# One of eight tiles transposed by PE inside a product, in a spectral filter, soft mixture and SoLU kernel

## The chip, the cores and the metric

The kernel runs on one core of one Trainium2 chip. Its engines are PE (the matmul array, with its weight loads listed apart as PEld), DVE (vector), ACT (scalar), POOL (GpSimd) and SP, which here only issues DMAs. Each engine takes its instructions in the order in which the program lists them and waits on semaphores where data come from another. The metric is device microseconds; the time is the median of several runs.

## The reference

```
X = rfft(x over 3072 positions)          # x: 8 x 3072 x 256
Y = softshrink(complex X @ (w_r, w_i) + b);  x = irfft(Y)     # 24576 tokens of 256
# soft mixture: 32 slots of 8 experts, dispatch and combine by softmax of x @ phi
x = combine @ experts(dispatch.T @ x)    # w1, w2 with relu
h = x @ w_in                             # 24576 x 1024
solu = h * softmax(h)
ln = (solu - mean) / sqrt(var + 1e-6) * g_ln
out = ln @ w_out                         # 24576 x 256
```

## The kernel before

A first phase (to some 660 us of the profile) does the filter, the statistics of the mixture and the combine weights, which it writes to memory as c. The change lies in the second phase, the function phase2: 192 tiles of 128 tokens. The experts' outputs times w_in are one 128 x 1024 matrix (gst), so a tile's hidden values are one product of c with it.

For a tile t these are the operations, with the name of the function that issues them:
- hmat: two matmuls of 512 columns into hps, 128 x 1024 in PSUM. There are three such buffers.
- rowmax (DVE): a reduction over hps. gst has its sign turned, so the minimum is taken.
- expo (ACT): the exponential e of hps, with its sum.
- umul (DVE): u = hps times e, with its sum. It is the last reader of hps.
- vari (ACT): the square of u less its mean, only for its sum.
- blocks: DVE transposes u in blocks of 32 x 32 into tb, and SP issues four DMAs that move whole blocks within the chip's memory, so that t2 holds u with hidden features on partitions.
- uhi and ulo: f32 is split into a rounded part uh (f32r, ACT for 768 columns, POOL for 256) and a rest ul (POOL, two subtractions of 512 columns).
- prod: 24 matmuls of 256 columns into po, in f32r: uh with the high and with the low part of gw (w_out scaled by g_ln, split likewise), and ul with the high part. po holds two tiles to a buffer and has two buffers.
- rstd (POOL, four small operations to four tiles) and outp (ACT): the product scaled into osb; store writes four tiles' osb out.

The last two tiles are "direct": their u is transposed by PE (trans), for which the columns of their hidden values are put in another order by the matrix gstn. load_c brings c for coming tiles, four DMAs to eight tiles.

All this is issued from one hand-written loop. In step i it issues hmat(i+3), rowmax(i+2), umul(i+1), blocks(i+1), store, load_c, outp(i-6), vari(i), expo(i+2), uhi(i-1), ulo(i-1), rstd(i) and prod(i-3), and no scheduler changes the order. An engine therefore runs its part of this list in order, and a wait on it delays all that stands behind.

Of the kernel before, what the change touches and what calls it, by code (L numbers as in the profile page):

```python
# [8 lines left out]
F32 = mybir.dt.float32  # L9
F32R = mybir.dt.float32r  # L10
# [3 lines left out]
AF = mybir.ActivationFunctionType  # L14
ALU = mybir.AluOpType
# [20 lines left out]
def kernel(  # L36
# [24 lines left out]
    PE, ACT, DVE, POOL, SP = nc.tensor, nc.scalar, nc.vector, nc.gpsimd, nc.sync  # L61
    B, N, D = x.shape
# [5 lines left out]
    DFF = 1024  # L68
    NI = T // 128
# [18 lines left out]
    def mm(out, lhsT, rhs, start=True, stop=True):  # L88
        PE.matmul(out=out, lhsT=lhsT, rhs=rhs, start=start, stop=stop)  # L89

    def tp(out, in_, k=128):
        PE.transpose(out=out, in_=in_, identity=ident[0:k, 0:k])  # L92
# [752 lines left out]
    def phase2(p2: ExitStack, pw: ExitStack):  # L845
        k_p = p2.enter_context(tc.tile_pool(name="k2_p", bufs=1))
        c_p = p2.enter_context(tc.tile_pool(name="c_p", bufs=1))

        gw = k_p.tile([128, 8, 2, D], F32R, name="gw")
        gw_h, gw_l = gw[:, :, 0, :], gw[:, :, 1, :]  # L850
        gst = k_p.tile([128, DFF], F32R, name="gst")
        gstn = k_p.tile([128, DFF], F32R, name="gstn")
        cts = {}


# [8 lines left out]
        p = ExitStack()  # L864
# [5 lines left out]
        ps = pt.tile([128, 2, 32], F32, name="pslt", tag="pt")  # L870
# [66 lines left out]
        for fh in range(2):  # L937
            n = 0
# [13 lines left out]
        def right(name, bufs, **k):  # L952
            return p2.enter_context(tc.tile_pool(name=name, bufs=bufs, side="right", **k))

        e_p = right("e_p", 2)
        u_p = right("u_p", 4)
        o_p = right("o_p", 2)
# [3 lines left out]
        po_p = right("po_p", 2, space=PSUM)  # L961
        NG = NI // 4
        ctt, hps, et, ut, uht, stt, osb, pot = {}, {}, {}, {}, {}, {}, {}, {}
# [13 lines left out]
        def hmat(i):  # L977
            if i >= NI:
                return
            j, k = divmod(i, 4)  # L980
            ps = ph_p.tile([128, DFF], F32, name="hps", tag="hps")
            for fh in range(2):
                mm(ps[:, 512 * fh:512 * fh + 512], ctt[j][:, 128 * k:128 * k + 128], (gstn if direct(i) else gst)[:, 512 * fh:512 * fh + 512])
            hps[i] = ps

        def stats(i):
            j, k = divmod(i, 4)
            if k == 0 and j not in stt:
                stt[j] = s_p.tile([128, 6, 4], F32, name="st", tag="st")
            return stt[j], k  # L990

        def rowmax(i):
            if i >= NI:
                return
            st, k = stats(i)
            DVE.tensor_reduce(out=st[:, 0, k:k + 1], in_=hps[i], op=ALU.min, axis=AX.X)  # L996

        def expo(i):
            if i >= NI:
                return  # L1000
            st, k = stats(i)
            e = e_p.tile([128, DFF], F32, name="e", tag="e")
            ACT.activation(out=e, in_=hps[i], func=AF.Exp, bias=st[:, 0, k:k + 1], scale=-1.0, accum_out=st[:, 1, k:k + 1])  # L1003
            et[i] = e

        def umul(i):
            if i >= NI:
                return
            st, k = stats(i)
            u = u_p.tile([128, DFF], F32, name="u", tag="u")  # L1010
            DVE.scalar_tensor_tensor(out=u, in0=hps.pop(i), scalar=1.0, in1=et.pop(i), op0=ALU.mult, op1=ALU.mult, accum_out=st[:, 2, k:k + 1])  # L1011
            ut[i] = u


        def direct(i):
            return i >= NI - 2

        def gst_order():
            POOL.tensor_copy(out=gstn.rearrange("p (c j b) -> p b c j", c=8, b=4), in_=gst.rearrange("p (b c j) -> p b c j", b=4, c=8).bitcast(F32))

        def blocks(i):
            if i >= NI or direct(i):
                return
            t = u_p.tile([128, DFF], F32, name="tb", tag="tb", bufs=3)
            DVE.transpose(out=t, in_=ut[i])  # L1027
            t2 = u_p.tile([128, 4, 256], F32, name="t2", tag="t2", bufs=3)
            for a in range(4):
                z = slice(32 * a, 32 * a + 32)  # L1030
                SP.dma_start(out=t2[:, a, :], in_=t[z].rearrange("i (b x) -> i b x", b=4))  # L1031
            t2t[i] = t2

        def trans(i):
            if i >= NI or not direct(i):
                return
            ps = ph_p.tile([128, 8, 128], F32, name="pu", tag="hps")
            for c in range(8):
                tp(ps[:, c, :], ut[i][:, 128 * c:128 * c + 128])
            ut[i, 0] = ps  # L1040

        def parts(i):
            uh = u_p.tile([128, 8, 128], F32R, name="uh", tag="uh")
            ul = u_p.tile([128, 8, 128], F32R, name="ul", tag="ul")
            uht[i] = (uh, ul)
            return uh, ul
# [9 lines left out]
                DVE.tensor_tensor(out=ul[:, z, :], in0=ps[:, z, :], in1=uh[:, z, :].bitcast(F32), op=ALU.subtract)  # L1056


        HA = 6

        def uhi(i):
            if i < 0 or direct(i):
                return
            uh, ul = parts(i)
            v = t2t[i].rearrange("p a (c j) -> p c a j", c=8)
            w = uh.rearrange("p c (a j) -> p c a j", a=4)
            ACT.activation(out=w[:, 0:HA], in_=v[:, 0:HA], func=AF.Copy)  # L1067
            POOL.tensor_copy(out=w[:, HA:8], in_=v[:, HA:8])  # L1068

        def ulo(i, n):  # L1070
            if i < 0 or direct(i):
                return
            uh, ul = uht[i]
            z = slice(4 * n, 4 * n + 4)
            v = t2t[i].rearrange("p a (c j) -> p c a j", c=8)[:, z]
            w = uh[:, z, :].rearrange("p c (a j) -> p c a j", a=4)
            POOL.tensor_tensor(out=ul[:, z, :].rearrange("p c (a j) -> p c a j", a=4), in0=v, in1=w.bitcast(F32), op=ALU.subtract)  # L1077
            if n:
                t2t.pop(i)


        def vari(i):
            if i >= NI:
                return
            st, k = stats(i)
            sq = e_p.tile([128, DFF], F32, name="sq", tag="sq", bufs=1)
            ACT.activation(out=sq, in_=ut.pop(i), func=AF.Square, bias=st[:, 2, k:k + 1], scale=-float(DFF), accum_out=st[:, 3, k:k + 1])  # L1087

        def prod(i):
            if i < 0 or i >= NI:  # L1090
                return
            uh, ul = uht.pop(i)
            if i % 2 == 0:
                pot[i // 2, 0] = po_p.tile([128, 2, D], F32, name="po2", tag="po2")
            ps = pot[i // 2, 0][:, i % 2, :]
            for f in range(8):
                mm(ps, uh[:, f, :], gw[:, f, 0, :], f == 0, False)
                mm(ps, uh[:, f, :], gw[:, f, 1, :], False, False)
            for f in range(8):
                mm(ps, ul[:, f, :], gw[:, f, 0, :], False, f == 7)  # L1100
            pot[i] = ps


        def rstd(i):
# [9 lines left out]
            POOL.tensor_tensor(out=st[:, 3, k], in0=st[:, 3, k], in1=st[:, 1, k], op=ALU.add)  # L1114
            POOL.tensor_tensor(out=st[:, 4, k], in0=st[:, 3, k], in1=mhalf[:, k], op=ALU.pow)

        o_todo = {}

        def outp(i):
            if i < 0:  # L1120
                return
            j, k = divmod(i, 4)
            b, r = divmod(j, 6)
            h, ah = divmod(r, 2)
            v = out.rearrange("(b h lm a) d -> b h lm a d", b=B, h=3, a=8)[b, h, :, 4 * ah:4 * ah + 4, :]
            if k == 0:
                osb[0] = o_p.tile([128, 4, D], F32, name="osb", tag="osb")
            o = osb[0]
            ACT.activation(out=o[:, k], in_=pot.pop(i), func=AF.Copy, scale=stt[j][:, 4, k:k + 1])  # L1129
            if j == NG - 1:  # L1130

                SP.dma_start(out=v[:, k, :], in_=o[:, k, :])
            elif k == 3:
                o_todo[i + 2] = (v, o)


        def store(i):
            if i in o_todo:
                v, os2 = o_todo.pop(i)
                SP.dma_start(out=v, in_=os2)  # L1140
# [20 lines left out]
        def late_c(i):  # L1161
            if i in c_todo:
                load_c(*c_todo.pop(i))
# [5 lines left out]
        for i in range(3):  # L1169
            hmat(i)  # L1170
# [5 lines left out]
        blocks(0)  # L1176
        for i in range(NI + 6):
            j, k = divmod(i, 4)
            hmat(i + 3)
            trans(i)  # L1180
            rowmax(i + 2)
            umul(i + 1)
            blocks(i + 1)
            store(i - 6)
            late_c(i)
            last_c(i)
            outp(i - 6)
            vari(i)
            expo(i + 2)
            direct_parts(i)  # L1190
            if i <= NI:
                uhi(i - 1)
                ulo(i - 1, 0)
            rstd(i)
            if i <= NI:
                ulo(i - 1, 1)
            if i == 40:
                gst_order()
            if k == 1:
                pieces(j + 2)  # L1200
            prod(i - 3)
        while o_todo:
            store(min(o_todo))

# [139 lines left out]
```

## Time and profile before

| | |
|---|---|
| time, median of 3 runs | 1365.99 us (1365.64 to 1366.42) |
| profiled execution, first to last instruction | 1364.4 us |
| busy: PE, PEld, DVE, ACT, POOL | 1268.9, 1126.9, 1207.1, 1038.8, 979.4 us |
| mean granted clock of PE | 0.981 of 2.4 GHz |
| DMA, mean | 185 GB/s |

The profile is of one execution, and its own time is the span of 1364.4 us; the median of the runs is 1.6 us above it. The busy times are sums over the whole span, over two phases with different limits, so they do not say what bounds the second. A matmul's duration includes its way through the array; the distance between the starts of two is what each costs in a row of them. The same holds in part on DVE and ACT, whose instructions overlap a little.

### The profile page before, as it was taken

What the parts mean: (1) busy time and instruction counts of PE and PEld (TensorE: products, weight loads), DVE (VectorE), ACT (ScalarE), POOL (GpSimd) and SP (SyncE); (2) the same over time, 40 slices, a digit from 0 to 9 for tenths busy, and PEclk for the clock granted to TensorE, in tenths of its full rate; (3) what the DMA queues carried; (4) which work ended last, traced back from release to release, by engine and by line L of the source; (5) the groups of instructions that cost most, each with busy time, mean ns of one, the idle gap of its engine ahead of it and who ended that gap; (6) DMA issues with size and microseconds to landing.
All of it is one profiled execution on the core that took longest, in us unless ns stands there. A gap on an engine that the chain in (4) does not pass through costs nothing.

```text
span 1364.4 us, 30891 instructions
## 1 busy us (share of the span) xinstructions
PE 1268.9 (93%) x10784; PEld 1126.9 (83%) x10784; DVE 1207.1 (88%) x1691; ACT 1038.8 (76%) x2005; POOL 979.4 (72%) x1045
## 2 busy tenths in 40 slices
PE   6999999999999999878699989999999999899998
PEld 3888888888878788855588888988898889888897
DVE  7787988888888989765999999999999999999994
ACT  5567665666667665533799889999899999899995
POOL 5557575757565654221588989989899999889996
PEclk8899999999999999999799999999999999999999
DMA  8966463646445464168478788778877888787874
GB/s 267 289 202 175 124 193 111 209 117 186 140 144 167 126 181 155 62 223 291 108 179 220 188 210 209 198 197 209 205 194 203 196 198 217 196 206 191 201 197 125
DMA packets 190746, 252.70 MB, mean 185 GB/s; under 512 B 21504, under 2 KB 155392, under 8 KB 190592
## 3 DMA queue, kind: packets, MB, share of 16 engines
q1 hardware_dynamic: 190256, 249.57, 67.3%
q8 instruction: 85, 1.39, 0.4%
q10 hardware_dynamic: 336, 1.18, 0.2%
q14 instruction: 69, 0.57, 0.1%
HBM read 91.94 MB, written 59.11 MB: 111 GB/s over the span
## 4 chain that ended last, share of the span: by engine, by line
PE 37%; POOL 14%; DMA 13%; issue 12%; DVE 10%; SPq 8%; ACT 6%; POOLq 0%; ACTq 0%; DVEq 0%
PE po L89 10%; DMA t<-tb 9%; POOL ul L1077 8%; PE pb L89 6%; PE pm L89 6%; SPq L1031 6%; PE s L89 4%; PE xps L89 4%; PE pa L89 3%; DMA xc<-in_x_dram 3%; POOL x L235 2%; PE sps L92 2%; SPq L861 2%; POOL uh L1068 2%; ACT uh L1067 1%
## 5 line engine op out<-in xcount | busy, mean ns | idle before, releaser
L1077 POOL TENSOR_TENSOR ul<-t,uh 128x512 fp32r<-128x512 f32 x380 | 486.1, 1296 | 31.8 <-ACT uh L1067 30.7
L89 PEld LDWEIGHTS po<-gw,uh 128*128 128x128 f32 x3072 | 384.9, 190 | 80.8 <-ACT osb L1129 72.2
L89 PE MATMUL po<-gw,uh 128*128 128x256 f32 x3072 | 404.9, 284 | 41.7 <-ACT osb L1129 41.4
L346 POOL TENSOR_TENSOR s<-yb,s 128x512 f32<-128x512 f32 x95 | 132.4, 1394 | 216.9 <-DVE s L345 187.8
L1027 DVE STREAM_TRANSPOSE tb<-u 128x1024 f32<-128x1024 f32 x190 | 236.7, 1246 | 7.0 <-DMA t<-tb 0.4
L1011 DVE SCALAR_TENSOR_TENSOR u<-hps,e 128x1024 f32<-128x1024 f32 x192 | 232.3, 1210 | 11.6 <-ACT e L1003 11.1
L996 DVE TENSOR_REDUCE st<-hps 128x1 f32<-128x1024 f32 x192 | 227.7, 1186 | 1.7 <-PE hps L89 1.7
L1087 ACT ACTIVATE sq<-u,st 128x1024 f32<-128x1024 f32 x192 | 221.3, 1152 | 0.2 <-DVE u L1011 0.2
L1003 ACT ACTIVATE e<-hps,st 128x1024 f32<-128x1024 f32 x192 | 214.1, 1115 | 7.2 <-DVE st L996 6.6
L89 PE MATMUL po<-gw,ul 128*128 128x256 f32 x1536 | 213.0, 281 | 0.8 <-POOL ul L1077 0.8
L89 PEld LDWEIGHTS po<-gw,ul 128*128 128x128 f32 x1536 | 195.3, 189 | 1.1 <-POOL ul L1077 1.0
L1067 ACT ACTIVATE uh<-t 128x768 fp32r<-128x768 f32 x190 | 160.5, 845 | 44.6 <-DMA t<-tb 41.1
L235 POOL TENSOR_TENSOR x<-xc,x 96x512 fp32r<-96x512 f32 x120 | 164.7, 1381 | 29.5 <-ACT x L234 28.4
L89 PE MATMUL hps<-gst,ct 128*128 128x512 f32 x380 | 119.5, 397 | 12.0 <-DVE u L1011 10.5
L261 ACT ACTIVATE asb<-s 96x512 f32<-96x512 f32 x112 | 66.6, 595 | 73.8 <-PE s L89 73.2
L89 PE MATMUL s<-x,df_h 96*96 96x512 f32 x240 | 105.0, 440 | 12.9 <-ACT x L234 4.6
L1068 POOL CAST uh<-t 128x256 fp32r<-128x256 f32 x190 | 75.9, 400 | 49.9 <-DMA t<-tb 46.3
L89 PEld LDWEIGHTS xps<-d_sb,apt 128*128 128x128 f32 x768 | 99.4, 194 | 14.1 <-issue 2.9
L89 PE MATMUL xps<-d_sb,apt 128*128 128x128 f32 x768 | 105.8, 281 | 2.1 <-DMA apt<-ad 1.6
L1129 ACT ACTIVATE osb<-po,st 128x256 f32<-128x256 f32 x192 | 89.5, 468 | 10.2 <-PE po L89 9.1
L234 ACT ACTIVATE x<-xc 96x512 fp32r<-96x512 f32 x120 | 75.1, 626 | 13.2 <-DMA xc<-in_x_dram 13.2
L297 DVE TENSOR_TENSOR xsum<-xps,xi 128x256 f32<-128x256 f32 x96 | 39.8, 414 | 47.9 <-ACT xh L296 44.8
(204 smaller groups left out, 2232.1 us busy)
## 6 DMA issues: line engine op xcount, KB each, us to landing
t<-tb SPq DMA_DIRECT2D x760, 128.0 KB, 2.8
apt<-ad SPq DMA_DIRECT2D x96, 256.0 KB, 4.2
out_dram<-osb SPq DMA_DIRECT2D x47, 512.0 KB, 3.7
xc<-in_x_dram SPq DMA_DIRECT2D x56, 384.0 KB, 3.9
ad<-asb SPq DMA_DIRECT2D x56, 384.0 KB, 3.4
ct<-c_dram SPq DMA_DIRECT2D x96, 128.0 KB, 3.9
wt<-in_moe_w_dram SPq DMA_DIRECT2D x21, 512.0 KB, 8.8
ws<-in_moe_w_dram SPq DMA_DIRECT2D x22, 256.0 KB, 5.9
```

Source lines behind the costliest of these rows:

```text
L89: PE.matmul(out=out, lhsT=lhsT, rhs=rhs, start=start, stop=stop)
L235: POOL.tensor_tensor(out=lo, in0=t, in1=hi.bitcast(F32), op=ALU.subtract)
L346: (DVE if last else POOL).tensor_tensor(out=s, in0=y, in1=s, op=ALU.subtract)
L996: DVE.tensor_reduce(out=st[:, 0, k:k + 1], in_=hps[i], op=ALU.min, axis=AX.X)
L1003: ACT.activation(out=e, in_=hps[i], func=AF.Exp, bias=st[:, 0, k:k + 1], scale=-1.0, accum_out=st[:, 1, k:k + 1])
L1011: DVE.scalar_tensor_tensor(out=u, in0=hps.pop(i), scalar=1.0, in1=et.pop(i), op0=ALU.mult, op1=ALU.mult, accum_out=st[:, 2, k:k + 1])
L1027: DVE.transpose(out=t, in_=ut[i])
L1067: ACT.activation(out=w[:, 0:HA], in_=v[:, 0:HA], func=AF.Copy)
L1068: POOL.tensor_copy(out=w[:, HA:8], in_=v[:, HA:8])
L1077: POOL.tensor_tensor(out=ul[:, z, :].rearrange("p c (a j) -> p c a j", a=4), in0=v, in1=w.bitcast(F32), op=ALU.subtract)
L1087: ACT.activation(out=sq, in_=ut.pop(i), func=AF.Square, bias=st[:, 2, k:k + 1], scale=-float(DFF), accum_out=st[:, 3, k:k + 1])
L1129: ACT.activation(out=o[:, k], in_=pot.pop(i), func=AF.Copy, scale=stt[j][:, 4, k:k + 1])
```

## The change

Tiles 22, 30, and so on to 182 are "turned". The hidden values of a turned tile are made with gstn, its u is transposed by PE with eight transposes into its own hps buffer, and one ACT copy of 1024 columns takes them to the f32 tile raw. There is no block transpose and there are no moves for such a tile. Of its product four of the eight groups of 128 features are f32 matmuls of raw with gwf, the unsplit w_out; for the other four POOL makes the two f32r parts, and they take twelve f32r matmuls. gwf is made by four POOL sums in steps 10 to 16, and gstn in step 8 (before: step 40).

In all tiles: outp is issued for two tiles in each odd step, uhi and ulo for tile i-2 in step i (before i-1), prod for i-4 (before i-3), and the rings of t2 and uh are one buffer longer. The transposes of a turned tile are issued one step before its own, between the sixteenth and the seventeenth matmul of the running product, and in its own step twelve matmuls of the next product are issued ahead of hmat. In that step expo stands ahead of vari.

```diff
         gst = k_p.tile([128, DFF], F32R, name="gst")
-        gstn = k_p.tile([128, DFF], F32R, name="gstn")
         cts = {}
...
+        f_p = right("f_p", 1)
+        gwf = f_p.tile([128, 8, D], F32, name="gwf")
+        gstn = f_p.tile([128, DFF], F32R, name="gstn")
         e_p = right("e_p", 2)
...
             for fh in range(2):
-                mm(ps[:, 512 * fh:512 * fh + 512], ctt[j][:, 128 * k:128 * k + 128], (gstn if direct(i) else gst)[:, 512 * fh:512 * fh + 512])
+                mm(ps[:, 512 * fh:512 * fh + 512], ctt[j][:, 128 * k:128 * k + 128], (gstn if direct(i) or turned(i) else gst)[:, 512 * fh:512 * fh + 512])
             hps[i] = ps
...
             u = u_p.tile([128, DFF], F32, name="u", tag="u")
-            DVE.scalar_tensor_tensor(out=u, in0=hps.pop(i), scalar=1.0, in1=et.pop(i), op0=ALU.mult, op1=ALU.mult, accum_out=st[:, 2, k:k + 1])
+            DVE.scalar_tensor_tensor(out=u, in0=hps[i] if turned(i) else hps.pop(i), scalar=1.0, in1=et.pop(i), op0=ALU.mult, op1=ALU.mult, accum_out=st[:, 2, k:k + 1])
             ut[i] = u
...
+        def turned(i):
+            return i % 8 == 6 and 16 < i < NI - 2
+
         def gst_order():
...
+        def gw_sum(n):
+            z = slice(2 * n, 2 * n + 2)
+            POOL.tensor_tensor(out=gwf[:, z], in0=gw[:, z, 0].bitcast(F32), in1=gw[:, z, 1].bitcast(F32), op=ALU.add)
+
         def blocks(i):
-            if i >= NI or direct(i):
+            if i >= NI or direct(i) or turned(i):
                 return
...
             DVE.transpose(out=t, in_=ut[i])
-            t2 = u_p.tile([128, 4, 256], F32, name="t2", tag="t2", bufs=3)
+            t2 = u_p.tile([128, 4, 256], F32, name="t2", tag="t2", bufs=4)
             for a in range(4):
...
         def parts(i):
-            uh = u_p.tile([128, 8, 128], F32R, name="uh", tag="uh")
+            uh = u_p.tile([128, 8, 128], F32R, name="uh", tag="uh", bufs=5)
             ul = u_p.tile([128, 8, 128], F32R, name="ul", tag="ul")
...
+        def turn(i):
+            ps = hps.pop(i).rearrange("p (c j) -> p c j", c=8)
+            for c in range(8):
+                tp(ps[:, c, :], ut[i][:, 128 * c:128 * c + 128])
+            raw, hl = parts(i)
+            ACT.activation(out=raw.bitcast(F32), in_=ps, func=AF.Copy)
+
+        def turned_parts(i, n):
+            raw, hl = uht[i]
+            r = raw[:, 4:8].bitcast(F32)
+            if n == 0:
+                POOL.tensor_copy(out=hl[:, 0:4], in_=r)
+            else:
+                POOL.tensor_tensor(out=hl[:, 4:8], in0=r, in1=hl[:, 0:4].bitcast(F32), op=ALU.subtract)
+
         HA = 6
...
             if i < 0 or direct(i):
+                return
+            if turned(i):
+                turned_parts(i, 0)
                 return
...
             if i < 0 or direct(i):
+                return
+            if turned(i):
+                if n:
+                    turned_parts(i, 1)
                 return
...
-        def prod(i):
+        def prod(i, left=0):
             if i < 0 or i >= NI:
                 return
-            uh, ul = uht.pop(i)
-            if i % 2 == 0:
-                pot[i // 2, 0] = po_p.tile([128, 2, D], F32, name="po2", tag="po2")
-            ps = pot[i // 2, 0][:, i % 2, :]
-            for f in range(8):
-                mm(ps, uh[:, f, :], gw[:, f, 0, :], f == 0, False)
-                mm(ps, uh[:, f, :], gw[:, f, 1, :], False, False)
-            for f in range(8):
-                mm(ps, ul[:, f, :], gw[:, f, 0, :], False, f == 7)
-            pot[i] = ps
+            if i not in pr_ops:
+                uh, ul = uht.pop(i)
+                if i % 2 == 0:
+                    pot[i // 2, 0] = po_p.tile([128, 2, D], F32, name="po2", tag="po2")
+                ps = pot[i // 2, 0][:, i % 2, :]
+                if turned(i):
+                    ops = [(uh[:, f, :].bitcast(F32), gwf[:, f, :]) for f in range(4)]
+                    hi = [(f, ul[:, f - 4, :], ul[:, f, :]) for f in range(4, 8)]
+                else:
+                    ops = []
+                    hi = [(f, uh[:, f, :], ul[:, f, :]) for f in range(8)]
+                for f, h, _ in hi:
+                    ops += [(h, gw[:, f, 0, :]), (h, gw[:, f, 1, :])]
+                ops += [(l, gw[:, f, 0, :]) for f, _, l in hi]
+                pot[i] = ps
+                pr_ops[i] = [(ps, a, b, n == 0, n == len(ops) - 1) for n, (a, b) in enumerate(ops)]
+            ops = pr_ops[i]
+            while len(ops) > left:
+                mm(*ops.pop(0))
...
-        o_todo = {}
+        o_todo, pr_ops = {}, {}
...
         def outp(i):
-            if i < 0:
+            if i < 0 or i >= NI:
                 return
...
             j, k = divmod(i, 4)
+            if turned(i):
+                prod(i - 4, 12)
             hmat(i + 3)
...
             last_c(i)
-            outp(i - 6)
-            vari(i)
-            expo(i + 2)
+            if i % 2 == 1:
+                outp(i - 7)
+                outp(i - 6)
+            if turned(i):
+                expo(i + 2)
+                vari(i)
+            else:
+                vari(i)
+                expo(i + 2)
             direct_parts(i)
-            if i <= NI:
-                uhi(i - 1)
-                ulo(i - 1, 0)
+            if i <= NI + 1:
+                uhi(i - 2)
+                ulo(i - 2, 0)
             rstd(i)
-            if i <= NI:
-                ulo(i - 1, 1)
-            if i == 40:
+            if i <= NI + 1:
+                ulo(i - 2, 1)
+            if i == 8:
                 gst_order()
+            if i in (10, 12, 14, 16):
+                gw_sum(i // 2 - 5)
             if k == 1:
                 pieces(j + 2)
-            prod(i - 3)
+            if turned(i + 1):
+                prod(i - 4, 8)
+                turn(i + 1)
+            prod(i - 4)
         while o_todo:
...

```

The first place is PE in steps 21 and 22, where tile 22 is turned. hps is the hidden product, of which the first below is that of tile 24, and po2 the product into the output. Before:

```order
L89 MATMUL hps_10033<-gst_8777,ct_9329 128x512 x2
L89 MATMUL po2_10057<-gw_8776,uh_9947 128x256 x16
L89 MATMUL po2_10057<-gw_8776,ul_9948 128x256 x8
L89 MATMUL hps_10082<-gst_8777,ct_9329 128x512 x2
L89 MATMUL po2_10057<-gw_8776,uh_10003 128x256 x16
L89 MATMUL po2_10057<-gw_8776,ul_10004 128x256 x8
```

Now, where hps_9905 is tile 22 and hps_10077 tile 25:

```order
L89 MATMUL hps_10011<-gst_8777,ct_9301 128x512 x2
L89 MATMUL po2_9986<-gw_8776,uh_9926 128x256 x16
L92 MATMUL hps_9905<-ident_62,u_10015 128x128 x8
L89 MATMUL po2_9986<-gw_8776,ul_9927 128x256 x8
L89 MATMUL po2_10064<-gw_8776,uh_9980 128x256 x12
L89 MATMUL hps_10077<-gst_8777,ct_9301 128x512 x2
L89 MATMUL po2_10064<-gw_8776,uh_9980 128x256 x4
L89 MATMUL po2_10064<-gw_8776,ul_9981 128x256 x8
```

Between the hidden products of tiles 24 and 25 there are now 36 matmuls and eight transposes in place of 24 matmuls, and the buffer of tile 25 is the one that the transposes fill.

The second place is ACT in the same steps; uh<-t2 is the copy of moved blocks, osb the copy to the output, sq the squares and e the exponential. Before:

```order
L1003 ACTIVATE e_10049,st_9881<-hps_9982,st_9881 128x1024
L1067 ACTIVATE uh_10051<-t2_9936 128x768
L1129 ACTIVATE osb_10096<-po2_9957,st_9675 128x256
L1087 ACTIVATE sq_10098,st_9881<-u_10037,st_9881 128x1024
L1003 ACTIVATE e_10100,st_10085<-hps_10033,st_10085 128x1024
L1067 ACTIVATE uh_10102<-t2_9990 128x768
```

Now:

```order
L1169 ACTIVATE osb_9919<-po2_9880,st_9448 128x256 x2
L1118 ACTIVATE sq_10019,st_9859<-u_9964,st_9859 128x1024
L1005 ACTIVATE e_10021,st_9859<-hps_9960,st_9859 128x1024
L1094 ACTIVATE uh_10023<-t2_9865 128x768
L1073 ACTIVATE uh_10053<-hps_9905 128x1024
L1005 ACTIVATE e_10091,st_10080<-hps_10011,st_10080 128x1024
L1118 ACTIVATE sq_10093,st_9859<-u_10015,st_9859 128x1024
L1094 ACTIVATE uh_10095<-t2_9913 128x768
```

The copy of the transposed tile, hps_9905, is put between the copy of moved blocks and the next exponential, and the two output copies are neighbours.

The third place is DVE there; tb is the block transpose. Now:

```order
L998 TENSOR_REDUCE st_9859<-hps_9960 128x1
L1013 SCALAR_TENSOR_TENSOR u_10015,st_9859<-hps_9905,e_9978 128x1024
L998 TENSOR_REDUCE st_10080<-hps_10011 128x1
L1013 SCALAR_TENSOR_TENSOR u_10082,st_9859<-hps_9960,e_10021 128x1024
L1036 STREAM_TRANSPOSE tb_10084<-u_10082 128x1024
L998 TENSOR_REDUCE st_10080<-hps_10077 128x1
```

Before, a transpose stood behind each multiplication; behind that of tile 22 there is none now.

## Rows read from the trace of the kernel before

**Rows 1.** Window, length, then us busy: PE, PEld, DVE, ACT, POOL.

```profile
700.00:1340.00 640.00, 599.20 (x4597) 561.64 (x4595) 622.07 (x709) 593.95 (x1062) 584.62 (x719) 0.99 0.80 201
```

**Rows 2.** DVE's groups there: count, busy us, mean ns, idle before, releaser.

```profile
L1027 DVE STREAM_TRANSPOSE tb<-u 128x1024 f32<-128x1024 f32 x177 | 220.5, 1246 | 6.5 <-DMA t<-tb 0.4
L1011 DVE SCALAR_TENSOR_TENSOR u<-hps,e 128x1024 f32<-128x1024 f32 x177 | 214.2, 1210 | 10.6 <-ACT e L1003 10.0
L996 DVE TENSOR_REDUCE st<-hps 128x1 f32<-128x1024 f32 x178 | 211.1, 1186 | 0.8 <-PE hps L89 0.8
```

**Rows 3.** DVE in order of time: start, us, instruction.

```profile
1003.23 1.21 DVE L1011 SCALAR_TENSOR_TENSOR u<-hps,e 128x1024 f32<-128x1024 f32 x1
...
1004.48 1.25 DVE L1027 STREAM_TRANSPOSE tb<-u 128x1024 f32<-128x1024 f32 x1
1005.65 1.19 DVE L996 TENSOR_REDUCE st<-hps 128x1 f32<-128x1024 f32 x1
1006.76 1.21 DVE L1011 SCALAR_TENSOR_TENSOR u<-hps,e 128x1024 f32<-128x1024 f32 x1
```

**Rows 4.** Waits from 700 to 1340 us: total, times, longest.

```profile
PEld po L89 <- ACT osb L1129: 70.2, 84, 2.7
ACT uh L1067 <- DMA t<-tb: 40.7, 38, 2.4
```

**Rows 5.** SP's issues in order of time from 1000 us.

```profile
1000.23 8.51 SPq L1031 DMA_DIRECT2D t<-tb  x12
...
1009.49 2.45 SPq L861 DMA_DIRECT2D ct<-c_dram  x4
```

**Rows 6.** ACT and DVE in order of time (in brackets: idle before).

```profile
915.69 0.84 ACT L1067 ACTIVATE uh<-t 128x768 fp32r<-128x768 f32 x1 [1.33 <-issue]
...
919.15 1.23 DVE L1011 SCALAR_TENSOR_TENSOR u<-hps,e 128x1024 f32<-128x1024 f32 x1 [0.49 <-ACT e L1003]
```

**Rows 7.** PE in order of time from 1007 us.

```profile
1007.49 0.62 PE L89 MATMUL hps<-gst,ct 128*128 128x512 f32 x2
1007.94 2.04 PE L89 MATMUL po<-gw,uh 128*128 128x256 f32 x16
1009.82 1.10 PE L89 MATMUL po<-gw,ul 128*128 128x256 f32 x8
1010.76 0.62 PE L89 MATMUL hps<-gst,ct 128*128 128x512 f32 x2
```

**Rows 8.** Weight loads of a direct tile's eight transposes, at 1343 us.

```profile
1343.04 0.90 PEld L92 LDWEIGHTS pu<-ident,u 128*128 128x128 f32 x8
```

**Rows 9.** Two f32 matmuls of 256 columns, and their min/median/max ns.

```profile
311.65 0.60 PE L89 MATMUL pm<-q_sb,e_sb 128*128 128x256 f32 x2
...
L89 PE MATMUL pm<-q_sb,e_sb x2: 379/380/382, 311.6 to 311.9; 128*128 128x256 f32 x2
```

**Rows 10.** ACT in order of time, and 512-column copies as a group.

```profile
1006.08 0.84 ACT L1067 ACTIVATE uh<-t 128x768 fp32r<-128x768 f32 x1
...
1008.30 1.11 ACT L1003 ACTIVATE e<-hps,st 128x1024 f32<-128x1024 f32 x1
...
1009.39 0.85 ACT L1067 ACTIVATE uh<-t 128x768 fp32r<-128x768 f32 x1
...
L1055 ACT ACTIVATE uh<-pu 128x512 fp32r<-128x512 f32 x4 | 2.4, 600 | 1.6 <-DVE ul L1056 1.6
```

**Rows 11.** POOL in order of time from 1008 us.

```profile
1008.37 0.19 POOL L1112 TENSOR_SCALAR st<-st 128x4 f32<-128x4 f32 x1
...
1010.18 1.29 POOL L1077 TENSOR_TENSOR ul<-t,uh 128x512 fp32r<-128x512 f32 x1
1011.42 0.40 POOL L1068 CAST uh<-t 128x256 fp32r<-128x256 f32 x1
...
1014.26 0.42 POOL L1068 CAST uh<-t 128x256 fp32r<-128x256 f32 x1
```

**Rows 12.** PE's weight loads in the tail, at 1354 us.

```profile
1353.97 0.55 PEld L89 LDWEIGHTS po<-gw,ul 128*128 128x128 f32 x4 [1.01 <-POOL ul L1077]
```

## Prediction

> **What bounds the kernel now.** I read the busy time by stretch first. In the second phase, from 700 to 1340 us, DVE is busy 622 of 640 us, PE 599, ACT 594 and POOL 585 [rows 1]: DVE is the bound, and three engines stand within 6% of it. The groups of DVE instructions say how much it loses: 6.5 + 10.6 + 0.8 = 17.9 us of idle time over 177 tiles [rows 2], so a tile takes 640/177 = 3.616 us. DVE's own order of time gives the tile without idle: from one multiplication to the next 3.53 us, of which the block transpose holds 1.17 us (its start to the start of the reduction behind it, not its 1.25 us of duration) [rows 3]. Eight tiles are therefore 28.24 us of DVE work and 28.93 us of time.
>
> The waits name what disturbs DVE [rows 4]: ACT waits 40.7 us for the moved blocks, PE's weight loads 70.2 us for output copies, DVE 10.0 us for exponentials. They are one chain. SP needs 8.51 us for three tiles' twelve moves, and four loads of c, 2.45 us, stand between at times [rows 5]; the blocks then come late, ACT stands at its copy (1.33 us at 915.69), everything behind it on ACT is late, and DVE's multiplication at 919.15 has to wait 0.49 us for its exponential [rows 6].
>
> **The change part by part, per group of eight tiles.** Tiles 22, 30, ..., 182 are turned: 21 groups.
>
> *DVE* loses one block transpose: 28.24 - 1.17 = 27.07 us. Nothing is added to it. Over 21 groups: -24.6 us.
>
> *PE* without a wait needs 3.27 us a tile (hidden product to hidden product; 0.45 of it for the hidden product, 1.88 for the sixteen matmuls behind it, so 0.118 each) [rows 7]. A turned tile adds eight f32 transposes, which the tail shows: 0.90 us for eight [rows 8]. Its product becomes four f32 matmuls of 256 columns and twelve f32r ones, in place of twenty-four f32r. The nearest rows for f32 at 256 columns are the two of q_sb and e_sb: 0.60 us for both, of which 0.38 is one duration, so 0.22 each [rows 9]. That is 4 x 0.22 + 12 x 0.118 = 2.30 against 2.83, a saving of 0.53. PE's group: 8 x 3.27 - 0.53 + 0.90 = 26.5 us.
>
> Two f32r matmuls are 0.236, so by the row f32 costs about two passes. The Trainium skill ("FP8 and Floating Point Precision", TensorE Precision Notes) says that true FP32 takes four passes through the array. By that rule four passes at this case's 0.118 would be 0.47 each, PE's group 27.5 us, above DVE's; the row contradicts it, and I keep it only as a rival.
>
> *ACT* needs 3.31 us a tile (copy to copy), with one copy of 768 columns in 0.84 [rows 10]. A turned tile puts in its place one copy of 1024 columns out of PSUM, not in the trace at that size. Bounds: 0.84, what 768 columns take; 1.20, two copies of 512 out of PSUM at 0.60 [rows 10]. I take 1.1, which is 0.84 x 1024/768. ACT's group: 8 x 3.31 - 0.84 + 1.1 = 26.7 us. The output copies keep their number and size.
>
> *POOL* needs 2.84 us a tile, and 1.81 for the four small operations of every fourth: 3.29 [rows 11], 26.3 us a group. A turned tile replaces a cast of 256 and two subtractions of 512 by a cast of 512 (at most two of 256 at 0.40) and one subtraction (1.29): 0.75 less. The sums that make gwf are four operations of 512, at most 1.3 each, in steps 10 to 16: 5 us of POOL where it has 0.24 us a tile to spare. The product is used two steps after its parts are made, against two before as well, but the blocks now have one step more before they are asked for, and four buffers; I cost these sums at nothing; if that cover is gone they cost up to 5 us. The move of gst_order from step 40 to 8 is the same instruction earlier.
>
> *SP* issues four moves fewer for a turned tile. Nothing of it is moved past anything except that stores stay where they were, two steps behind the copies.
>
> So after the change DVE still has the most work, 27.07, but PE 26.5, ACT 26.7 and POOL 25.5 are within 1.6 us of it over eight tiles. What decides is how the turned step is coupled.
>
> **The turned step.** Its hidden-product buffer goes back not when DVE has multiplied, but after eight transposes and ACT's copy; and PE is given twenty matmuls between the transposes and the next hidden product. From the end of DVE's multiplication of the turned tile, PE's way to the next hidden product that DVE has to reduce is 0.90 + 20 x 0.118 + 0.62 for the hidden product itself, 3.88, with some 0.1 for two signals 3.98 us. DVE's own way to that reduction is a reduction (1.11), a multiplication (1.25) and a transpose (1.17): 3.53. So DVE waits 0.45 us in each group, if PE stands ready when the multiplication ends: 21 x 0.45 = 9.5 us. It can be ready: a group at 27.07 + 0.45 = 27.52 leaves PE 1.0 us over its 26.5, and the wait for output copies goes away (the pair is copied a step before PE asks for the buffer). ACT's copy comes behind the same transposes and ahead of one exponential (1.11) [rows 10]: 0.90 + 1.1 + 1.11 = 3.1, and DVE asks for that exponential one more reduction after its 3.53, at 4.64.
>
> *The stalls.* One step more before the blocks are wanted (3.53 us) is longer than the longest wait for them, 2.4 [rows 4], so ACT's 40.7 us should go, and with them DVE's waits for exponentials, 10.0 of the 17.9. The other 7.9 I leave. Bounds: nothing, and all 17.9.
>
> *The tail.* The product stands one step later, so one more of 2.83 us follows the last tile; PE's wait for POOL there, 1.01 us [rows 12], goes: +1.8.
>
> Sum on the profiled execution, span 1364.4: -24.6 + 9.5 - 10.0 + 1.8 = -23.3, so 1341.1. The median of the runs is 1.6 above the span: **1342.7 us**.
>
> **Rivals.**
> 1. *PE comes late to the transposes* (slower). Its place is PE's queue in the step before a turned tile: the transposes stand behind the hidden product and sixteen matmuls. Before, the hidden product at 1007.49 starts 3.0 us after the multiplication that frees its buffer has ended (1003.23 + 1.21) [rows 3, 7]. Add 0.45 + 1.88, and PE reaches the transposes 5.3 us after that end, where the next multiplication has ended after 3.53: 1.8 late. Then DVE waits 0.45 + 1.8 a group, 27.07 + 2.25 = 29.32 against 28.93: +8 us, with the tail 1376; if the old stalls (0.69 a group) stay on top, +14 more, 1390. It decides once PE's lateness exceeds 1.4 us a group. For it: with PE and ACT at 96% and more of 27.5 there is little with which to catch up. Against: PE's lateness comes from the waits that should go.
> 2. *ACT is the bound.* It has 0.3 us a group to spare. If its copy waits for the transposes as long as PE is late, 1.5 us, ACT needs 28.2 a group, and 0.7 x 21 = 15 us are won: with the tail 1353. For it: of the 46 us that ACT is not busy in the stretch [rows 1], 40.7 are one wait [rows 4], so it has hardly any other slack. Against: the copy is asked for late in a step, behind an exponential and another copy.
> 3. *No price for the turned step and no stall left*: -24.6 - 17.9 + 1.8, 1325.
> 4. *f32 at four passes*: PE 27.5 and the 0.45 at the turned step, about 28.0 a group: 0.93 x 21 = 19.5 less than before, with the tail 1348. For it speaks that rule of the Trainium skill; against it [rows 9].
>
> **How the numbers follow.** My forecast, with anything from none to all of the waits on exponentials gone and a price of the step from 0.2 to 0.8, reaches from 1333 to 1352; I give it 0.52. Rival 1 gets 0.18 (1368 to 1390), rival 2 0.18 (1350 to 1366), rival 3 0.08, rival 4 0.04. The range from 1327 to 1372 leaves out the lower part of rival 3 and the upper part of rival 1. About 0.2% (2.7 us) is what a measurement of this kernel can tell from no change. Faster: all of the forecast, 3 and 4, and most of rival 2, 0.76; same: what of rival 2 and the low end of rival 1 comes near, 0.06; slower 0.18.
>
> **What would show it.** DVE's transposes number 169, and its busy time falls by about 25 us. If I am right, a turned tile's group takes about 27.5 to 27.9 us, DVE's wait for PE's hidden product grows from 0.8 to some 10 us in the row of the reductions, ACT's wait for moved blocks and PE's wait for output copies nearly vanish, and eight transposes into the hidden product take 0.9 us. Rival 1 shows as over 1.5 us of wait per group before the reduction; rival 2 as ACT idle before its 1024-column copy and DVE idle before its multiplications; rival 4 as f32 matmuls 0.47 apart. I am wrong if DVE's idle time grows by more than the 24.6 us that it loses in work.

## The result, and the profile after

The changed kernel takes 1344.66 us (median of 4 runs, 1343.49 to 1349.49) against 1366.2 of the kernel before beside it: a ratio of 0.9833, 95% interval 0.9813 to 0.9854. The forecast was 1342.7. The profiled execution spans 1341.9 us (1364.4 before).

The row that answers to [rows 1] (only to 1300 us, since the tiles end earlier), and the groups of DVE that answer to [rows 2] (to 1320 us):

```profile
700.00:1300.00 600.00, 594.72 (x4563) 572.87 (x4562) 580.80 (x671) 582.93 (x1038) 552.77 (x685) 1.00 0.76 191
```

```profile
L1013 DVE SCALAR_TENSOR_TENSOR u<-hps,e 128x1024 f32<-128x1024 f32 x179 | 216.5, 1209 | 0.3 <-ACT e L1005 0.3
L998 DVE TENSOR_REDUCE st<-hps 128x1 f32<-128x1024 f32 x177 | 211.4, 1195 | 12.5 <-PE hps L89 12.5
L1036 DVE STREAM_TRANSPOSE tb<-u 128x1024 f32<-128x1024 f32 x156 | 194.3, 1246 | 6.9 <-DMA t<-tb 1.5
```

DVE no longer waits for exponentials (10.0 us before, 0.3 now) and waits instead for hidden products (0.8, now 12.5). PE is busy in 594.7 of 600 us, 99%, against 599.2 of 640, 94%: it has become the fullest engine, which I had not forecast. The waits from 700 to 1320 us answer to [rows 4]; columns are the total, how often, and the longest:

```profile
DVE st L998 <- PE hps L89: 12.5, 22, 1.8
...
PEld po L89 <- POOL ul L1108: 6.9, 8, 2.2
...
ACT uh L1094 <- DMA t<-tb: 1.1, 1, 1.1
```

ACT's 40.7 us for moved blocks are 1.1, and PE's 70.2 us for output copies are no longer in the list. Now DVE, then PE and ACT, in order of time through one turned step:

```profile
1011.07 1.21 DVE L1013 SCALAR_TENSOR_TENSOR u<-hps,e 128x1024 f32<-128x1024 f32 x1
1012.21 1.22 DVE L998 TENSOR_REDUCE st<-hps 128x1 f32<-128x1024 f32 x1
1013.34 1.21 DVE L1013 SCALAR_TENSOR_TENSOR u<-hps,e 128x1024 f32<-128x1024 f32 x1
1014.60 1.25 DVE L1036 STREAM_TRANSPOSE tb<-u 128x1024 f32<-128x1024 f32 x1
1016.31 1.23 DVE L998 TENSOR_REDUCE st<-hps 128x1 f32<-128x1024 f32 x1 [0.47 <-PE hps L89]
```

```profile
1010.45 2.04 PE L89 MATMUL po<-gw,uh 128*128 128x256 f32 x16
1012.35 1.09 PE L92 MATMUL hps<-ident,u 128*128 128x128 f32 x8
1013.20 1.20 PE L89 MATMUL po<-gw,ul 128*128 128x256 f32 x8
1014.23 1.59 PE L89 MATMUL po<-gw,uh 128*128 128x256 f32 x12
1015.66 0.62 PE L89 MATMUL hps<-gst,ct 128*128 128x512 f32 x2
...
1027.84 1.89 PE L89 MATMUL po<-gwf,uh 128*128 128x256 f32 x8
1029.38 1.78 PE L89 MATMUL po<-gw,ul 128*128 128x256 f32 x12
1031.00 0.62 PE L89 MATMUL hps<-gstn,ct 128*128 128x512 f32 x2
...
1039.94 1.09 PE L92 MATMUL hps<-ident,u 128*128 128x128 f32 x8
```

```profile
1013.52 1.03 ACT L1073 ACTIVATE uh<-hps 128x1024 f32<-128x1024 f32 x1 [0.25 <-issue]
```

From transposes to transposes a group of eight tiles is 27.59 us (28.93 before; 27.5 to 27.9 forecast), and DVE waits 0.47 (0.45 forecast) at the reduction behind the turned step. But PE goes from its sixteenth matmul straight into the transposes, without the spare time that I gave it. The reason stands at 1027.84: four f32 matmuls are eight records, and a turned tile's product takes 3.16 us (1027.84 to 1031.00), not 2.30.

A measure freed of the first phase (whose end moves by some us from run to run) is the loop, from DVE's first reduction to its last multiplication. The first line of each pair is of before, the second of after; the last numbers are first and last start:

```profile
L996 DVE TENSOR_REDUCE st<-hps x192: 1182/1185/1225, 651.8 to 1339.2; 128x1 f32<-128x1024 f32 x192
L1011 DVE SCALAR_TENSOR_TENSOR u<-hps,e x192: 1205/1208/1226, 654.3 to 1342.4; 128x1024 f32<-128x1024 f32 x192
```

```profile
L998 DVE TENSOR_REDUCE st<-hps x192: 1184/1186/1226, 650.3 to 1313.4; 128x1 f32<-128x1024 f32 x192
L1013 DVE SCALAR_TENSOR_TENSOR u<-hps,e x192: 1205/1208/1225, 652.8 to 1316.0; 128x1024 f32<-128x1024 f32 x192
```

The loop went from 690.6 to 665.7 us, 24.9 less; the tail behind it from 22.0 to 25.9, 3.9 more; and the loop began 1.5 us earlier, which is of the first phase.

### The profile page after: what moved, and what is told of

Read it like the earlier page. It is cut to its first block, busy times and chain, and to the rows that moved or that the text cites. A ratio compares the mean times of both kernels' runs of the same rounds, so it can differ in the third digit from the quotient of the medians.

```text
span 1341.9 us, 30708 instructions
## 1 busy us (share of the span) xinstructions
PE 1278.4 (95%) x10868; PEld 1152.1 (86%) x10868; DVE 1181.0 (88%) x1670; ACT 1042.3 (78%) x2005; POOL 962.0 (72%) x1028
## 4 chain that ended last, share of the span: by engine, by line
PE 72%; DVE 11%; POOL 6%; issue 5%; DMA 3%; ACT 2%; SPq 1%; POOLq 0%; DVEq 0%; ACTq 0%
PE po L89 36%; PE pb L89 7%; PE pm L89 6%; PE hps L89 6%; PE s L89 5%; PE xps L89 4%; PE pa L89 3%; POOL ul L1108 2%; POOL x L235 2%; PE sps L92 2%; DMA xc<-in_x_dram 2%; PE hps L92 1%; PE pm L92 1%; DVE xl L298 1%; DVE yb L339 1%
## 5 line engine op out<-in xcount | busy, mean ns | idle before, releaser
L1108 POOL TENSOR_TENSOR ul<-t,uh 128x512 fp32r<-128x512 f32 x338 | 433.3, 1299 | 37.2 <-ACT uh L1094 35.2
L89 PEld LDWEIGHTS po<-gw,uh 128*128 128x128 f32 x2736 | 348.7, 189 | 14.0
L89 PE MATMUL po<-gw,uh 128*128 128x256 f32 x2736 | 354.9, 281 | 0.0
L89 PE MATMUL po<-gw,ul 128*128 128x256 f32 x1620 | 231.2, 285 | 7.4 <-POOL ul L1108 7.1
L1036 DVE STREAM_TRANSPOSE tb<-u 128x1024 f32<-128x1024 f32 x169 | 210.5, 1246 | 7.3 <-DMA t<-tb 1.5
L89 PEld LDWEIGHTS po<-gw,ul 128*128 128x128 f32 x1620 | 207.0, 188 | 10.8 <-POOL ul L1108 9.4
L1094 ACT ACTIVATE uh<-t 128x768 fp32r<-128x768 f32 x169 | 143.4, 849 | 1.1 <-DMA t<-tb 1.1
L89 PE MATMUL hps<-gst,ct 128*128 128x512 f32 x338 | 107.5, 401 | 14.3 <-DVE u L1013 12.9
L1095 POOL CAST uh<-t 128x256 fp32r<-128x256 f32 x169 | 68.4, 405 | 37.9 <-DMA t<-tb 37.9
L1169 ACT ACTIVATE osb<-po,st 128x256 f32<-128x256 f32 x192 | 80.3, 476 | 11.4 <-PE po L89 11.4
```

## The experiments

All are edits of the changed kernel. "Ratio" is to the kernel before on the same chip; its medians there were 1366.2 to 1368.7 us, so ratios compare better than medians.

| | median us | ratio, 95% | loop us |
|---|---|---|---|
| changed kernel | 1344.66 | 0.9833 (0.9813 to 0.9854) | 665.7 |
| no tile turned | 1359.36 | 0.9929 (0.9912 to 0.9946) | 679.3 |
| turned alone | 1364.67 | 0.9978 (0.9962 to 0.9995) | 692.3 |
| one pass for f32 | 1343.93 | 0.9828 (0.9808 to 0.9848) | 664.6 |
| hidden product first | 1351.58 | 0.9881 (0.9862 to 0.9900) | 672.3 |
| both of these | 1334.54 | 0.9756 (0.9738 to 0.9775) | 655.6 |
| no pairs | 1346.68 | 0.9844 (0.9825 to 0.9863) | 666.1 |
| sums early | 1342.76 | 0.9817 (0.9798 to 0.9837) | 662.7 |
| eight ahead | 1343.37 | 0.9817 (0.9798 to 0.9836) | 663.5 |
| early and eight ahead, 22 tiles | 1339.72 | 0.9782 (0.9758 to 0.9806) | 659.9 |
| the same, two f32 groups | 1339.14 | 0.9777 (0.9752 to 0.9802) | 657.4 |
| one in four | 1365.32 | 0.9974 (0.9959 to 0.9989) | 686.4 |

A loop time is of the one profiled execution. Up to the first transposes of a turned tile, "one pass for f32" does the same work as the changed kernel, yet that part of its loop took 84.3 us against 83.2; so 1 us between two loops tells nothing. A group is steadier: from the third on, those of the changed kernel lie between 27.51 and 27.60 us.

**The two halves apart.** No tile turned (and the sums for gwf left out, gstn in step 40 again):

```diff
-            return i % 8 == 6 and 16 < i < NI - 2
+            return False
```

> No tile is turned; the later blocks and products, the paired output copies and the longer rings stay. If the later step takes away DVE's waits for exponentials (10.0 of 17.9 us of idle time before) and lengthens the tail by 4 us, DVE alone bounds it at 3.53 us a tile: 1355 to 1361 us. Rival, that the later step is worth nothing by itself and only makes room for the turned tiles: 1364 to 1368.

The time falls in the first range. DVE's groups from 700 to 1300 us show no wait for an exponential or a hidden product:

```profile
L1036 DVE STREAM_TRANSPOSE tb<-u 128x1024 f32<-128x1024 f32 x169 | 210.5, 1246 | 9.4 <-DMA t<-tb 2.7 <-DVE u L1013 1.0
L1013 DVE SCALAR_TENSOR_TENSOR u<-hps,e 128x1024 f32<-128x1024 f32 x169 | 204.1, 1208 | 0.0
L998 DVE TENSOR_REDUCE st<-hps 128x1 f32<-128x1024 f32 x169 | 200.3, 1185 | 0.0
```

The loop of 679.3 us is near 192 x 3.53 = 677.8, which is DVE's work alone, and 11.3 us shorter than before. So the later steps, with the paired copies and the longer rings, are worth that alone (10.0 forecast); the step and the longer rings were not tried apart. The turned tiles alone:

```diff
-                prod(i - 4, 12)
+                prod(i - 3, 12)
...
-            if i % 2 == 1:
-                outp(i - 7)
-                outp(i - 6)
+            outp(i - 6)
...
-                uhi(i - 2)
-                ulo(i - 2, 0)
+                uhi(i - 1)
+                ulo(i - 1, 0)
...
-            prod(i - 4)
+            prod(i - 3)
```

> Turned tiles stay; moved blocks, products and output copies are put back to their steps of before (parts of i-1, product of i-3, one output copy a step). If the lead is what keeps PE and ACT in time, the old waits for moved blocks and output copies come back and a group of eight takes 28.3 to 29.3 us in place of 27.6: 1358 to 1378 us. Rival, that the transposes saved on DVE are the whole gain: within 3 us of the changed kernel, 1342 to 1348.

The lead is what counts: the time is in the first range, and the loop (692.3 us) is not shorter than before. The runs scatter from 1362 to 1373 and the profiled one is of the longer (span 1367.4), so the 0.2% of the ratio says little; the waits, 700 to 1300 us, and one group (PE, DVE, PE) say more:

```profile
PEld po L89 <- ACT osb L1169: 38.9, 60, 3.3
ACT uh L1094 <- DMA t<-tb: 33.5, 22, 3.0
...
DVE st L998 <- PE hps L89: 27.5, 22, 2.8
DVE u L1013 <- ACT e L1005: 10.1, 13, 3.4
```

```profile
1001.68 1.04 PE L92 MATMUL hps<-ident,u 128*128 128x128 f32 x8
...
1028.05 1.21 DVE L1013 SCALAR_TENSOR_TENSOR u<-hps,e 128x1024 f32<-128x1024 f32 x1
...
1030.93 1.03 PE L92 MATMUL hps<-ident,u 128*128 128x128 f32 x8
```

The old waits are back, and DVE's waits for hidden products are 1.25 us each (27.5 over 22) in place of 0.57 (12.5 over 22). This group takes 29.25 us; the twenty take from 27.9 to 32.9, 29.1 on average. The turned tile's multiplication ends at 1029.26 and its transposes start 1.7 us later: PE late at the transposes, the slower rival (1.8 there), is what the turned tiles meet without the lead. By the loops of the profiled runs the halves give 11.3 us and nothing, together 24.9; by the ratios they give 0.7% and 0.2%, together 1.7%.

**Coupling or PE's own work.** By "coupling" I mean the turned step's way from DVE's multiplication over PE's transposes and the twenty matmuls to the next hidden product. One pass:

```diff
-            ACT.activation(out=raw.bitcast(F32), in_=ps, func=AF.Copy)
+            ACT.activation(out=raw, in_=ps, func=AF.Copy)
...
-                    ops = [(uh[:, f, :].bitcast(F32), gwf[:, f, :]) for f in range(4)]
+                    ops = [(uh[:, f, :], gw[:, f, 0, :]) for f in range(4)]
```

> In turned tiles the four f32 matmuls become four f32r ones with the rounded u and the high part of the weights (the low parts of these are left out of the result). Theory A, PE's own work of 27.4 to 27.6 us bounds a group: PE falls by about 1.1 to 26.4, and the group falls until the next limit. Theory B, the twenty matmuls between transposes and the next hidden product bound it: DVE 27.07 + 0.45 stays, so the group stays at 27.5 and the time falls by at most 2 us. By A without B: 27.1 a group, 10 us less, 1334 to 1337.

Theory B: no change. PE is relieved, and waits; DVE waits as before (PE, then DVE, in order of time):

```profile
1012.82 1.09 PE L92 MATMUL hps<-ident,u 128*128 128x128 f32 x8 [0.91 <-DVE u L1013]
...
1040.42 1.09 PE L92 MATMUL hps<-ident,u 128*128 128x128 f32 x8 [0.91 <-DVE u L1013]
```

```profile
1016.79 1.23 DVE L998 TENSOR_REDUCE st<-hps 128x1 f32<-128x1024 f32 x1 [0.47 <-PE hps L89]
```

The group stays at 27.60. Hidden product first:

```diff
-            if turned(i):
-                prod(i - 4, 12)
             hmat(i + 3)
```

> In a turned tile's own step the hidden product is issued ahead of the twelve matmuls of the next product, so that eight and not twenty matmuls lie between the transposes and it. Theory B: DVE's wait of 0.45 us a group goes, 8 to 10 us less, 1334 to 1337. Theory A, PE's own work bounds the group: no wait of DVE there, but it stays at 27.5 (wait moved to another reduction), 1342 to 1347; a little slower if PE now waits for ACT's copy.

Neither number: 7 us slower, and of the expectation only its last clause came. Fewer matmuls stand behind the transposes, but PE now waits for ACT's copy (0.42 us before its weight load), and since PE has nothing to spare the group grows to 27.99 (PE, ACT and DVE in order of time):

```profile
1015.59 1.03 PE L92 MATMUL hps<-ident,u 128*128 128x128 f32 x8
1016.71 1.03 ACT L1073 ACTIVATE uh<-hps 128x1024 f32<-128x1024 f32 x1 [1.12 <-POOL uh L1095]
1017.79 0.30 PEld L89 LDWEIGHTS hps<-gst,ct 128*128 128x128 f32 x2 [0.42 <-ACT uh L1073]
...
1018.56 1.23 DVE L998 TENSOR_REDUCE st<-hps 128x1 f32<-128x1024 f32 x1 [0.41 <-PE hps L89]
```

(The releaser named in ACT's row, a POOL cast, is not what it waited for; the transposes end at 1016.62.) So fewer matmuls behind the transposes can help only while PE stands ready for them. Both edits together:

> Both edits together: one f32r pass with the rounded u in place of the f32 matmuls in turned tiles (low parts left out of the result), and the hidden product ahead of the next product. Each alone ran into the other limit: with PE's work at 26.4 us PE can stand ready, and with eight matmuls behind the transposes DVE need not wait, so a group comes to DVE's own 27.07 to 27.2 us: 9 to 11 us less than the changed kernel, 1333 to 1336. Rival, that ACT or the hold of the hidden buffer bounds it next: 1342 to 1351.

```profile
1008.29 1.09 PE L92 MATMUL hps<-ident,u 128*128 128x128 f32 x8 [0.21 <-DVE u L1013]
...
1035.41 1.09 PE L92 MATMUL hps<-ident,u 128*128 128x128 f32 x8 [0.20 <-DVE u L1013]
```

A group is 27.12 us, near DVE's own work (28.24 - 1.26 = 26.98, where 1.26 is what the missing transpose saves by the rows of the result), and the loop 10.1 us shorter. ACT is as full there as DVE (590.0 and 590.6 us busy of the 600 from 700 on), so which of the two would bound it next is not shown. Two limits of nearly the same height, PE's own work and the coupling, stood in the changed kernel; taking away either shows the other. Eight ahead, a smaller step:

```diff
-                prod(i - 4, 12)
+                prod(i - 4, 16)
```

> Eight and not twelve matmuls of the next product go ahead of the hidden product in a turned step (sixteen in place of twenty behind the transposes). The way from DVE's multiplication to the hidden product is 0.47 us shorter, so DVE's wait there falls from 0.47 to about 0. If PE's own work then bounds the group, at 27.4 to 27.5, the time falls by 2 to 4 us: 1340 to 1343; if only the coupling did, by 9: 1335. If PE runs into ACT's copy instead, no change or worse.

```profile
1015.45 1.03 PE L92 MATMUL hps<-ident,u 128*128 128x128 f32 x8
1042.94 1.03 PE L92 MATMUL hps<-ident,u 128*128 128x128 f32 x8
```

27.49 a group, in which PE shows no wait: that is PE's own work. The loop is 2.2 us shorter. DVE still waits 0.35 there and not about 0, since the transposes now start 0.5 us after the multiplication has ended (1013.74 + 1.21): PE comes late. The time alone (1343.37) can't be told from that of the changed kernel.

**The smaller parts.** One output copy in every step:

> Only the pairs are undone: one output copy in every step, as before; all else as changed. If the later product is what frees PE from waiting for output copies, nothing changes: 1342 to 1348 us. If the pairs are: on even steps PE asks for an output buffer whose second copy stands in the same step on ACT, and PE, which has no idle time in the changed kernel, loses up to 1 us for two tiles: 1350 to 1400.

The pairs are worth nothing that these runs can tell: the loop is 0.4 us longer, and the intervals overlap. ACT then waits 9.9 us for products where it waited for none; DVE's waits for exponentials come to no more than 2.2 us, and a group stays at 27.6 us. The sums early:

```diff
-            if i == 8:
-                gst_order()
-            if i in (10, 12, 14, 16):
-                gw_sum(i // 2 - 5)
...
+        for n in range(4):
+            gw_sum(n)
+        gst_order()
```

> The four POOL sums for gwf and the reordering of gstn are issued ahead of the first tile, where POOL stands idle, and no longer in steps 8 to 16. PE's two waits of 1.3 and 2.0 us for POOL's subtractions and DVE's wait of 1.5 us near 726 us should go: 2 to 4 us less, 1340 to 1343. Rival, that these waits are made up later by slack: no change.

As expected: PE's wait for subtractions at 700 to 1300 us falls from 6.9 us to the 1.6 below, and the loop by 3.0. The intervals of the times overlap.

```profile
PEld po L89 <- POOL ul L1108: 1.6, 2, 1.4
```

**More turned tiles, and a better version.** One in four:

> One tile in four is turned, the rest as changed. By PE's own work: four tiles at 3.27 and 1.2 us for a turned one are 14.3 us, so eight take 28.6, 1.0 more than with one in eight: over 21 groups of eight 21 us more, 1362 to 1368. By DVE's work, if that still bounded it: 25.9 to 26.8 us for eight, 1310 to 1330.

```profile
1005.46 1.03 PE L92 MATMUL hps<-ident,u 128*128 128x128 f32 x8
...
1019.82 1.03 PE L92 MATMUL hps<-ident,u 128*128 128x128 f32 x8
```

Four tiles take 14.36 us, as PE's work says (14.3): 28.7 for eight. DVE waits 57 us for hidden products from 700 to 1300 us. Two versions that leave nothing out:

> The sums for gwf ahead of the first tile, eight matmuls ahead of the hidden product, and tile 14 turned as well (22 turned tiles). If the two edits add up (2 and 1 us) and one more group is won (1.0): 1339 to 1342 us. A group stays at 27.5 us, PE's own work.

> As the kernel with early sums and eight matmuls ahead, but two of eight feature groups of a turned tile go in f32 and six in f32r with both parts, made by POOL. The f32 matmuls cost 1.54 us a tile for four groups against 1.42 in f32r for twelve matmuls and the product 3.16 against 2.83 us, so two groups fewer save PE 0.17 us a turned tile: a group of 27.3 us, 22 x 0.17 = 3.6 us less than with four: 1335.5 to 1338.5. POOL gets 0.8 us more a turned tile, within its slack; if it has none left, it is slower than with four groups: 1341 to 1346.

```profile
1010.79 1.03 PE L92 MATMUL hps<-ident,u 128*128 128x128 f32 x8
...
1026.19 1.02 PE L89 MATMUL po<-gwf,uh 128*128 128x256 f32 x4
...
1038.12 1.03 PE L92 MATMUL hps<-ident,u 128*128 128x128 f32 x8
```

These rows are of the second. The first adds up as expected, 5.8 us off the loop. With two feature groups in f32, eight tiles take 27.33 us in place of 27.49 (0.17 expected, 0.16 measured) and the loop is 2.5 us shorter; the time misses its range by 0.6; in the profiled run the loop began 1.2 us later, which is of the first phase. Both beat the changed kernel; they can't be told from each other by time.

## Why the prediction was right

- **DVE's lost transpose, -24.6, and the price of the turned step, 9.5.** Right, each a little small: two multiplications stand 2.27 us apart where no transpose is between (1011.07 and 1013.34), so 1.26 is saved and not 1.17; DVE's wait is 0.47, and the reduction starts 0.54 later than behind another transpose, for 0.45. The 0.1 for two signals, for which I had no row, holds: the multiplication ends at 1012.28 and the transposes start at 1012.35, the hidden product ends at 1016.28 and the reduction starts at 1016.31. That the coupling is real, and not only PE's slowness, is shown by the one-pass run, where PE stands ready and DVE waits the same.
- **PE's group of 26.5 us.** Wrong. I took two trace records for two f32 matmuls; they were one. [rows 9] are the record pair of one q_sb and e_sb product: the program has 16 of this shape, the trace of before 32 records. An f32 matmul of 256 columns costs (3.16 - 12 x 0.118)/4 = 0.435 us here, 3.7 f32r matmuls. The Trainium skill ("FP8 and Floating Point Precision", TensorE Precision Notes) has four passes for true FP32, and the trace agrees nearly (0.47 by that rule). PE's group is 8 x 3.27 + 0.33 + 0.85 = 27.3 by this sum. The eight-ahead run, where PE shows no wait, has 27.49; a part of the difference is that the eight matmuls behind the transposes take 1.03 us (1013.20 to 1014.23) and not 0.94. The 1.0 us to spare was not there.
- **Why the time came out all the same.** The two limits run beside each other, so the higher counts and not their sum: PE's 27.5 does not exceed what the coupling asks, 27.5 to 27.6. Rival 4 had the right premise and the wrong arithmetic, since it added DVE's 0.45 to PE's full queue. That the two came out so close is luck: 1 us more of PE's work, and the same mistake would have cost 21 us. The smaller misses below also cancel in part.
- **The stalls, -10.0.** Right in kind and nearly in size: 11.3 without turned tiles. The slower rival needed PE to be late; the lead removed that, as the turned-alone run shows. ACT as the bound (rival 2) did not come: its copy takes 1.03 us (1.1 estimated) and waits 0.25, and DVE's waits for exponentials are 0.3 us in all.
- **The POOL sums at nothing.** Mis-sized: 3.0 us, inside the bound of 5. They made PE wait 1.3 and 2.0 us for POOL's subtractions and DVE 1.5 us, and this was not made up. Of the 3.0, 1.5 lie ahead of the first turned tile's transposes and 1.4 in the first two groups.
- **The tail, +1.8.** Mis-sized: +3.9. One more product follows, as said, but PE's wait for POOL did not go; it grew from the 1.01 of [rows 12] to 2.5 us (waits of the changed kernel from 1300 us):

```profile
PEld po L89 <- POOL ul L1108: 2.5, 2, 1.4
```

By parts, then (the transposes of the turned tiles, first and last start):

```profile
L92 PE MATMUL hps<-ident,u x168: 270/273/330, 733.5 to 1289.1; 128*128 128x128 f32 x168
```

The last start is that of the eighth transpose of the last turned tile, whose first starts at 1288.2. So the 20 groups between take 554.8 us and, at 28.93, took 578.6: -23.8. The average of 27.74 is above 27.59 because of the second, 30.34 (761.39 to 791.73), in which PE waits 0.44 and 1.22 us for POOL's subtractions; the early-sums run brings it only to 29.31, so the sums are not all of its length. The rest of the loop gives -1.1, the tail +3.9, and the first phase -1.5: -22.5, the difference of the two spans.

## What to carry to other kernels

Before costing a matmul by a row of the trace, count its records against the instructions of the program: one f32 matmul instruction here leaves two (84 of them with gwf, 168 records). When work is moved from the fullest engine to another, compute both engines' sums for the period first: here, with one turned tile in n, 3.53 n - 1.26 for DVE and 3.27 n + 1.2 for PE cross at about n = 9, and one in four lost nearly all of the gain. And where an edit of one limit gives nothing, try it together with an edit of the next before dropping it: alone they gave nothing that can be told and -7 us here, together 10 (with a part of the result left out, so it is a test and not a version).

## What the runs showed of the hardware

Eight f32 transposes of 128 x 128 take 0.85 us on PE, one record each (0.79 in the eight-ahead run, where they start late). With the 0.09 more that the eight matmuls behind them take they cost no more than eight f32r matmuls of 256 columns (0.118 each); only the f32 products are dear, 0.435 us each. An ACT copy of 1024 f32 columns out of PSUM takes 1.03 us (600 ns for 512 in [rows 10], there into f32r).
